# Ten, nine and seven instead of eight, twelve and six: where 26 weight conversions run in an attention, expert and mixing kernel

## The chip, the cores and the metric

One core of one Trainium2 chip. The metric is the time of one execution in microseconds (us) on the device. Before: 499.5 us, the median of 3 runs (498.26 to 500.18).

## What is computed

Three layers one after the other, on a batch of 2 sequences of 768 tokens, 8 heads of 64 (so 512 channels). First attention in a window with a few global positions; then a layer of 8 experts, in which every token goes through one expert chosen by a scan over the sequence; then a mixing layer. The last two matter here:

```python
# experts (E = 8, F = 1024); e is the expert of the token
h = np.maximum(x[b, s] @ w1[e], 0.0)
out[b, s] = p[e] * (h @ w2[e])

# mixing layer
theta = x @ w_theta
zr, zi = x * np.cos(theta), x * np.sin(theta)
y = np.einsum('ts,bsd->btd', w_tok_r, zr) + np.einsum('ts,bsd->btd', w_tok_i, zi)
u = x + y
return u + np.maximum(u @ w_ch, 0.0)
```

## The kernel before

The weights of the mixing layer (`w_theta`, `w_tok` and `w_ch`) come to the kernel as 64-bit numbers. Each has to be turned into two 32-bit parts, a high one in the format of the matmul and the rest, before PE can use it. This is cut into 26 conversions of 128 x 512 numbers, the list `jobs` (L358): 0 to 3 are `w_theta`, 4 to 21 `w_tok` (three for each of six slices of 128 tokens), 22 to 25 `w_ch`. Nothing needs them before the mixing layer, so most of them are slipped in among the work of the experts.

One conversion is the generator `job` (L396): an absolute value on ScalarE (ACT, L408) and a shift on VectorE (DVE, L409); three more DVE steps that put the 32-bit number together (L411, L413, L415), with a `yield` between the steps; a pause of `lag` yields; the copy of the high part on ACT (L418) together with the issue of a later load (`job_load`, L381); and the subtraction for the low part on DVE (L421). `job_tick` (L423) takes an open conversion one step further, or begins the next one if its data has been asked for. `job_upto(n)` (L433) ticks until n conversions have been begun and none is open.

The kernel is scheduled by hand: each engine runs its instructions in the order of the program, so a conversion step stands in the queue of DVE or ACT exactly where its tick is called.

The experts are one loop over 64 units (L1539), eight for each expert. The unit u does the second product of unit u (`mm2`) and the first of unit u + 2 (`mm1`) on PE, splits the next weights into two parts on ACT and DVE (`split_w1`, for the first four experts alone, and `split_w2`), and applies the relu. Between these stand five ticks. Whether a unit ticks is asked once, from the number of conversions begun and a due line: `NJ1` conversions over the units up to 32, `NJ2` over the 25 units after that, between `J0 = 6` and `JL = 61`. Here `lag` is 5, so a conversion takes 10 ticks, and the raw data has room for two. The loads of the expert weights are issued by the SP queue, those of the conversions by ACT's.

The mixing layer takes what is left (L1781). A pass k (1 to 11) on PE is: a quarter of the token product of slice k (`h_mix`, L1729), the theta product of slice k + 2 (L1653), the transposes of slice k + 3 (L1617), the other three quarters. The theta product and the transposes write PSUM tiles of one pool `pB` with two buffers in turn. On DVE and ACT a pass is `trig_a` (L1663 on ACT, L1665 to L1671 on DVE) that reads theta, `h_xh` and `h_xl` that read the transposes, then sine, cosine and the two-part factors `z` (L1704, L1709). In pass 5 `h_u` (L1741, L1748) takes the sums of the first batch out of their six PSUM banks, which the first quarter of pass 6 writes again. The ticks of a pass are 18, in three places (`T1`, `T2`, `T3` = 2, 2, 14), and each is worth `nj / JT` of a step, where `nj` is the number of conversions left and `JT` = 18. Here `lag` is 1, so a conversion takes 6 steps. At the beginning of passes 1 to 5 stands a `job_upto` (L1879), which makes sure that the slice's weights are there. The conversions of this part have three buffers for raw data; the first three loads are issued by ACT's queue, the rest by SP's.

Of the kernel before, what the change touches and what calls it, by code (L numbers as in the profile page):

```python
# [49 lines left out]
BLOCKS = [b * NT + t for t in range(NT) for b in range(B)]  # L50
TWO_PI = 6.283185307179586

NJ1, NJ2 = 8, 12
NWARM = 8
WPS = 1
TR_LAST = {}
# [1922 lines left out]
```

## Time and profile before

| | before |
|---|---|
| median of 3 runs | 499.5 us (498.26 to 500.18) |
| the profiled execution | 502.46 us, its span 500.6 us |
| PE busy | 475.2 us, 95% of the span |
| DVE busy | 348.0 us, 70% |
| ACT busy | 265.7 us, 53% |
| experts in the trace | about 133 to 318 us, their second half from about 232 us |
| mixing layer | about 318 to 500 us |

PE is TensorE, PEld its loading of weights, DVE is VectorE, ACT ScalarE, POOL GpSimd, SP the queue of SyncE. A name such as L415 is line 415 of the kernel. Times in the rows are microseconds from the start of the span. Busy time of PE includes matmuls that overlap, so a stretch in which PE has no idle time is one in which it sets the pace.

### The profile page before, as it was taken

The page shows a single profiled execution, that of the slowest core. Times are in us where ns is not written, and L with a number is a line of the kernel's source. Part 1 is how long each engine was busy: PE and PEld are TensorE (multiplying, and loading weights), DVE is VectorE, ACT ScalarE, POOL GpSimd, SP SyncE. Part 2 cuts the span into 40 slices and gives each one's busy share as a digit, 9 for nine tenths or more (in the row PEclk, how much of TensorE's full clock was granted, in tenths as well). Part 3 has the DMA queues.
Part 4 walks back from the last instruction along what each step waited for, and adds up shares of the span by engine and source line. Part 5 has one row for each costly group of instructions (what it writes and reads, how often), then busy time and mean ns, then how long its engine had stood idle before and what let it go on. Part 6 is the DMA issues. An engine that isn't in the chain of part 4 may idle for free.

```text
span 500.6 us, 9754 instructions
## 1 busy us (share of the span) xinstructions
PE 475.2 (95%) x3424; PEld 393.5 (79%) x3424; DVE 348.0 (70%) x963; ACT 265.7 (53%) x647; POOL 145.0 (29%) x164
## 2 busy tenths in 40 slices
PE   8888998999899899999999989999999999999997
PEld 4567776668788689788888767888888888888886
DVE  6687776855577897976799888556888787571522
ACT  4877877572345776564656556446555354340300
POOL 6535463421401330201312101212443244250300
PEclk9899999899999999999999999999999999999999
DMA  8547575188898998687999984150221000000022
GB/s 274 180 129 259 150 246 196 38 252 282 301 260 161 373 321 288 212 275 232 291 309 347 345 272 133 52 185 1 84 65 63 22 22 22 0 1 33 31 106 84
DMA packets 53252, 86.33 MB, mean 172 GB/s; under 512 B 6512, under 2 KB 28784, under 8 KB 53200
## 3 DMA queue, kind: packets, MB, share of 16 engines
q1 hardware_dynamic: 44068, 63.25, 38.8%
q10 hardware_dynamic: 6380, 15.50, 9.9%
q0 software_dynamic: 2752, 6.93, 4.9%
q8 instruction: 28, 0.46, 0.4%
q14 instruction: 24, 0.20, 0.1%
HBM read 71.17 MB, written 14.49 MB: 171 GB/s over the span
## 4 chain that ended last, share of the span: by engine, by line
PE 57%; DMA 7%; DVE 5%; ACT 2%; issue 1%; ACTq 0%; DVEq 0%
PE a L1729 20%; PE o L1458 9%; PE h L1419 7%; PE b L1766 7%; PE th L1653 6%; DMA jraw<-in_w_tokT_dram 4%; PE h L1403 4%; DMA raw<-in_w_dram 3%; PE o L1469 2%; DVE w2s L1387 1%; PE b L1617 1%; DVE jw L413 1%; PE tr L1258 1%; PE th L1818 1%; DVE jw L415 1%
## 5 line engine op out<-in xcount | busy, mean ns | idle before, releaser
L1729 PE MATMUL a<-wtok,z 128*128 128x512 f32 x576 | 105.4, 341 | 0.0
L1729 PEld LDWEIGHTS a<-wtok,z 128*128 128x128 f32 x576 | 88.5, 188 | 13.1 <-DVE z L1709 0.3
L1458 PE MATMUL o<-w2s,hh 128*128 128x512 f32 x192 | 66.1, 419 | 3.8 <-ACT w2s L1386 1.9
L1419 PE MATMUL h<-xT,w1s 128*128 128x288 f32 (+3 forms) x384 | 52.7, 285 | 4.5 <-DVE w1s L1284 3.3
L1419 PEld LDWEIGHTS h<-xT,w1s 128*128 128x128 f32 x384 | 49.1, 190 | 8.4 <-DVE w1s L1284 4.6
L623 ACT ACTIVATE pr<-sm,st 128x256 f32<-128x256 f32 (+1 forms) x96 | 46.0, 483 | 14.7 <-DVE xt L696 12.1
L1387 DVE TENSOR_TENSOR w2s<-raw,w2s 128x512 fp32r<-128x512 f32 x64 | 43.9, 687 | 4.7 <-ACT w2s L1386 4.3
L1403 PE MATMUL h<-xT,raw 128*128 128x192 f32 (+1 forms) x256 | 44.4, 317 | 0.9 <-issue 0.9
L613 DVE CUSTOM_DVE_ANT_0 sm<-s,bias 128x256 f32<-128x256 f32 (+1 forms) x96 | 34.2, 394 | 14.1 <-PE s L589 13.0
L1403 PEld LDWEIGHTS h<-xT,raw 128*128 128x128 f32 x256 | 39.6, 190 | 4.9 <-issue 3.0
L1386 ACT ACTIVATE w2s<-raw 128x512 fp32r<-128x512 f32 x64 | 39.8, 622 | 3.7 <-ACT yo L1508 1.8
L1458 PEld LDWEIGHTS o<-w2s,hh 128*128 128x128 f32 x192 | 32.6, 186 | 10.4 <-DVE w2s L1387 4.6
L1051 POOL DMA_INDIRECT xg<-xd,xidx x17 | 16.9, 994 | 80.4 <-PE tr L1258 57.8
L1458 PE MATMUL o<-w2s,hl 128*128 128x512 f32 x96 | 37.9, 395 | 0.0
L1433 ACT ACTIVATE hh<-h 128x128 fp32r<-128x128 f32 (+3 forms) x64 | 20.4, 319 | 30.4 <-PE h L1419 15.2
L646 PE MATMUL pt<-ident,pr 128*128 128x128 f32 x176 | 27.2, 286 | 4.3 <-ACT ps L655 3.7
L1685 POOL TENSOR_TENSOR si<-si,yg 128x512 f32<-128x512 f32 x10 | 13.5, 1353 | 59.2 <-ACT si L1678 50.0
L655 ACT ACTIVATE ps<-pt 128x512 f32<-128x512 f32 (+1 forms) x44 | 24.6, 559 | 6.9 <-PE pt L646 6.9
L1774 DVE SCALAR_TENSOR_TENSOR ob<-b,xTf 128x512 f32<-128x512 f32 (+1 forms) x16 | 8.8, 556 | 27.7 <-PE b L1766 27.7
L1284 DVE TENSOR_TENSOR w1s<-raw,w1s 128x512 fp32r<-128x512 f32 x32 | 22.0, 689 | 8.1 <-ACT w1s L1283 7.8
L646 PEld LDWEIGHTS pt<-ident,pr 128*128 128x128 f32 x176 | 20.1, 145 | 8.7 <-ACT ps L655 5.7
L670 PE MATMUL x<-ps,vv 128*64 128x128 f32 x352 | 25.5, 281 | 0.2 <-ACT ps L655 0.2
(264 smaller groups left out, 949.7 us busy)
## 6 DMA issues: line engine op xcount, KB each, us to landing
raw<-in_w_dram SPq DMA_DIRECT2D x64, 512.0 KB, 6.4
qk<-in_pack_dram SPq DMA_DIRECT2D x11, 576.0 KB, 6.0
jraw<-in_w_tokT_dram ACTq DMA_DIRECT2D x12, 512.0 KB, 6.0
vv<-in_pack_dram SPq DMA_DIRECT2D x10, 512.0 KB, 4.4
w<-in_w_dram SPq DMA_DIRECT2D x16, 256.0 KB, 5.6
yd<-zero SPq DMA_DIRECT2D x13, 256.0 KB, 3.0
xd<-xt SPq DMA_DIRECT2D x12, 256.0 KB, 4.6
jraw<-in_w_tokT_dram ACTq DMA_DIRECT2D x12, 256.0 KB, 4.9
```

Of the source, the lines that this page charges most:

```text
L613: V.tensor_tensor_reduce(out=sm[:, hh, 0:W], in0=ust[u]["s"][hh][:, 0:W], in1=bias[:, 2 * j + hh], scale=-0.125, scalar=BIG, op0=ALU.add, ...
L623: A.activation(pr[:, hh, 0:W], sm[:, hh, 0:W], AF.Exp, bias=st[:, hh : hh + 1], scale=-1.0, accum_out=sums[n][:, 2 * j + hh : 2 * j + hh + 1],
L646: PE.transpose(pt[:, hh, c], pr[:, hh, c * 128 : (c + 1) * 128], ident)
L670: PE.matmul(xp[64 * hh : 64 * hh + 64, j], lhsT=vv[:, i, h * 64 : (h + 1) * 64], rhs=ps[:, hh, c], start=(c == 0), stop=(c == nch - 1),)
L1386: A.activation(h2, bb[:, o], AF.Copy)
L1387: V.tensor_tensor(l2, bb[:, o], f32(h2), op=ALU.subtract)
L1403: PE.matmul(hp[:, :N], lhsT=pieces[u // 2][1][:, j, o * 128 : (o + 1) * 128], rhs=x[:, j, :N], start=(j == 0), stop=(j == 3),)
L1419: PE.matmul(hp[:, :N], lhsT=wa[:, j], rhs=xa[:, j, :N], start=(k == 0), stop=(k == 11))
L1458: PE.matmul(out[:M], lhsT=ha[:, lo : lo + M], rhs=wa, start=(f == 0 and q == 0), stop=(f == 7 and q == 2),)
L1653: PE.matmul(th, lhsT=xa[:, j], rhs=wa[:, j], start=(n == 0), stop=(n == 11))
L1729: PE.matmul(acc[b][d][o], lhsT=za[:, d * 128 : (d + 1) * 128], rhs=wa[:, c, lo:hi], start=(t == 0 and n == 0 and (o == 0 or d % 2 == 0)), ...
L1766: PE.matmul(op[:, : hi - lo], lhsT=wa[:, d, e * 128 : (e + 1) * 128], rhs=ua[:, d, lo:hi], start=(n == 0), stop=(n == 11),)
```

## The change

```diff
-NJ1, NJ2 = 8, 12
+NJ1, NJ2 = 10, 9
```

Nothing else is edited. `NJ1` and `NJ2` stand in the due line (L1541), in the limit of `job_load` (L383) and in the assertions at the end of the experts (L1593). Written out, with the ticks that the rule gives:

| | before | after |
|---|---|---|
| units with ticks, first half (6 to 31) | 6 to 10, 12, 13, 16, 17, 20, 21, 24, 25, 28, 29 | 6 to 14, 16, 17, 20, 21, 23, 24, 26, 27, 29, 30 |
| units with ticks, second half (32 to 57) | 32, 33, 35 to 57 | 32, 33, 35, 36, 38, 39, 41, 42, 44 to 47, 49, 50, 52, 53, 55 to 57 |
| conversions begun before unit 32 / in the experts | 8 / 20 | 10 / 19 |
| left for the mixing layer (`nj`) | 6 | 7 |
| steps in a pass of the mixing layer | 6 | 7 |

## Rows read from the trace of the kernel before

**Rows 1.** Busy time by stretch: us, PE, PEld, DVE, ACT, POOL, granted clock, DMA, GB/s

```profile
150.00:232.00 82.00, 78.61 (x535) 68.55 (x535) 66.22 (x123) 52.52 (x108) 18.30 (x18) 1.00 0.88 275
232.00:310.00 78.00, 73.29 (x485) 60.32 (x484) 66.00 (x163) 45.44 (x100) 12.91 (x13) 1.00 0.84 279
343.40:390.50 47.10, 47.10 (x259) 40.29 (x258) 37.02 (x58) 25.52 (x45) 20.81 (x15) 1.00 0.18 57
...
165.00:185.00 20.00, 17.66 (x110) 14.96 (x109) 17.40 (x33) 14.08 (x29) 7.01 (x7) 1.00 1.04 356
```

**Rows 2.** Waits of PE, 150 to 232 us: us in total, times, longest

```profile
PE h L1419 <- DVE w1s L1284: 3.3, 4, 1.0
```

**Rows 3.** Waits of PE, 232 to 318 us

```profile
PE o L1458 <- ACT w2s L1386: 1.9, 2, 1.4
PE o L1458 <- DVE w2s L1387: 1.6, 4, 0.8
PE h L1403 <- issue: 0.9, 1, 0.9
```

**Rows 4.** Chain that ended last, mixing layer: start us, us, what

```profile
367.00 2.81 PE th L1653 x12
...
378.73 2.81 PE th L1653 x12
...
390.46 2.81 PE th L1653 x12
...
393.70 8.48 PE a L1729 x48
```

**Rows 5.** DVE in order of time, mixing layer: start, us, instruction, [idle before <- releaser]

```profile
361.73 0.69 DVE L1667 SCALAR_TENSOR_TENSOR rr<-kk,th 128x512 f32<-128x512 f32 x1
...
364.11 0.42 DVE L409 TENSOR_SCALAR jw<-jraw 128x512 int32<-128x512 int32 x1
...
366.62 0.69 DVE L411 SCALAR_TENSOR_TENSOR jw<-jraw,jw 128x512 int32<-128x512 int32 x1
367.46 1.54 DVE L1709 TENSOR_TENSOR z<-kk,z 128x512 fp32r<-128x512 f32 x1 [0.16 <-ACT z L1704]
368.92 0.68 DVE L413 SCALAR_TENSOR_TENSOR jw<-jraw,jw 128x512 int32<-128x512 int32 x1
369.63 0.69 DVE L415 SCALAR_TENSOR_TENSOR jw<-jm,jw 128x512 f32<-128x512 f32 x1
371.03 0.69 DVE L421 TENSOR_TENSOR wtok<-jw,wtok 128x512 fp32r<-128x512 f32 x1 [0.70 <-ACT wtok L418]
...
372.09 0.69 DVE L1667 SCALAR_TENSOR_TENSOR rr<-kk,th 128x512 f32<-128x512 f32 x1
...
382.66 0.69 DVE L1667 SCALAR_TENSOR_TENSOR rr<-kk,th 128x512 f32<-128x512 f32 x1
...
388.69 1.27 DVE L1709 TENSOR_TENSOR z<-kk,z 128x512 fp32r<-128x512 f32 x1 [0.44 <-ACT z L1704]
...
395.74 0.69 DVE L1741 TENSOR_TENSOR xTf<-a,xTf 128x512 f32<-128x512 f32 x1 [2.47 <-PE a L1729]
396.35 0.75 DVE L1748 TENSOR_TENSOR xTf<-a,xTf 128x256 f32<-128x256 f32 x2
```

**Rows 6.** DMA issues of the page: KB each, median us to landing

```profile
jraw<-in_w_tokT_dram ACTq DMA_DIRECT2D x12, 512.0 KB, 6.0
```

**Rows 7.** ACT, DVE and PE in order of time, second half of the experts

```profile
298.51 0.67 ACT L408 ACTIVATE jw<-jraw 128x512 f32<-128x512 f32 x1 [2.00 <-DMA jraw<-in_w_tokT_dram]
...
306.79 0.70 DVE L415 SCALAR_TENSOR_TENSOR jw<-jw 128x512 f32<-128x512 f32 x1
...
308.15 0.51 PE L1458 MATMUL o<-w2s,hh 128*128 128x512 f32 x1 [0.83 <-DVE w2s L1387]
```

**Rows 8.** DVE and PE in order of time, first half of the experts

```profile
209.97 0.69 DVE L415 SCALAR_TENSOR_TENSOR jw<-jw 128x512 f32<-128x512 f32 x1
...
211.32 1.49 PE L1419 MATMUL h<-xT,w1s 128*128 128x224 f32 x11 [1.04 <-DVE w1s L1284]
```

## The prediction

> **What bounds the kernel now.** I began with the busy time of the engines in three stretches [rows 1]. The reader is to see in them that TensorE (PE) is busy 78.61 of 82 us in the first half of the experts, 73.29 of 78 in the second and 47.10 of 47.10 in the last layer, at a granted clock of 1.00 throughout (the 2.4 GHz level), while VectorE (DVE) is the next busiest in all three. So PE is the floor, and a conversion can cost or give back only where PE waits. The waits of PE come next [rows 2, 3]: 3.3 us in the first half, all for `w1s` from DVE; 1.9 + 1.6 + 0.9 = 4.4 us in the second. For 326 to 497 us the same view lists none, and the chain of waits there is PE work end to end [rows 4]. Last I read DVE in order of time in the last layer [rows 5], because that gives the margin by which it runs ahead of PE.
>
> **What one conversion costs.** Its DVE instructions are L409 0.42 us, L411 0.69, L413 0.68, L415 0.69 and L421 0.69 [rows 5], together 3.17 us, plus two activations on ScalarE (ACT), L408 and L418, and one load of 512 KB that takes 6.0 us to land [rows 6]. The number of conversions in the kernel stays 26; all the change does is move them: two into the first half (+6.3 us of DVE), three out of the second (-9.5 us), one into the last layer (+3.2 us). Per-step dispatch, the number of loads and the engines that issue them stay, so these are costed at nothing.
>
> **Second half, three fewer.** Counting ticks by the rule at L1541, before has conversion steps in every unit from 35 to 57, after in 17 of these 23; in the last ten (48 to 57) before works on five conversions, after on about three and a half. In 232 to 310 us DVE is busy 66.00 of 78 us [rows 1], of which the twelve conversions are 12 x 3.17 = 38.0; without them PE would be far ahead as the bound, with them the two are near each other. The stalls have the conversion in front of them: at 306.79 us L415 ran ahead of the `w2s` subtraction (L1387) that PE then got at 308.15 after 0.83 us idle; at 298.51 us ACT had stood 2.00 us for `jraw` with the `w2s` copy queued behind it [rows 7]. In the last ten units the conversions ask 3.5 x 3.17 = 11.1 us of DVE where they asked 15.9, and most loads have three units instead of two until they are read. Bounds: at best all 4.4 us go, plus some 0.6 us by which single matmuls are stretched, 5.0; at worst what is left of the conversions still meets the output copies on ACT and half stays, 2.0. I take **-3.8 us**, near the upper end, because every one of the three waits has a conversion step or its load ahead of it.
>
> **First half, two more.** After has steps in units 6 to 14 without a gap, where before left out 11 and 14, and in ten of the units 11 to 24 instead of seven: 3 x 5 ticks, one and a half conversions, 4.8 us of DVE in less than half of the half. Over the whole of it DVE is busy 66.22 of 82 us [rows 1], 15.8 us idle, but part of that is waiting for ACT, which an in-order engine can't fill. The form of the stall is in the trace: L415 began at 209.97 us, the `w1s` subtraction stood behind it, and PE went on at 211.32 after 1.04 us idle [rows 8]. Two more conversions at such a stall each are 2.1 us. Bounds: 0.5 us if the idle time takes nearly all; 4.0 us if all but 0.8 of the 4.8 lands on PE. I take **+2.0 us**.
>
> **Last layer, one more: where I expect the change to be decided.** Six conversions shared by 18 ticks of a pass k give 6 steps a pass, and with a lag of 1 a conversion is exactly 6 steps: each begins and ends inside its pass. Seven give 7 steps: at the end of pass 1 the next conversion is begun (L409), and `job_upto` at L1879 doesn't only ask whether the number wanted has been begun, it runs on while a conversion is open. So passes 2, 3 and 4 each begin with the remaining five steps in one piece, ahead of `trig_a`; two conversions a pass instead of one, all seven done by pass 4 instead of pass 6. Each such piece, L409 included, holds DVE for 0.42 + 0.69 + 0.68 + 0.69 + 0.70 (the wait for ACT's copy) + 0.69 = **3.87 us** [rows 5]; behind it wait L1665 and all of `trig_a` on DVE, and on ACT the copy `kk`, since it stands behind L418.
>
> DVE has a margin to swallow this. It goes round in 372.09 - 361.73 = 10.36 us [rows 5], PE in 378.73 - 367.00 = 11.73 [rows 4]. The theta product of pass k+1 writes the PSUM tile (`pB`, two buffers shared with the transposes) that L1667 of pass k read last. Pass 2: L1667 ends at 361.73 + 0.69 = 362.42, theta begins at 367.00, margin 4.58; less 3.87 leaves 0.71, no wait. Pass 3: 378.73 - 372.78 = 5.95, less 7.74: PE waits 1.79. Pass 4: 390.46 - 383.35 = 7.11, less 11.61: 4.50 in all. Pass 5 evacuates the sums of the first batch: the bank that PE wants at 393.70 + 3/4 x 8.48 = 400.06 is free when L1748 ends, at 397.10. DVE's delay is then 11.61 less 2.47 (its idle before the second L1741, which it no longer has) and less 0.44 (its wait at 388.69, which was one for PE in the end) [rows 5], 8.70: 405.80 against 400.06 + 4.50, another 1.24. Sum **+5.7 us**. What is late next, the `z` parts, has more margin: pass 4's end at 388.69 + 1.27 = 389.96, 10.1 us before 400.06. From pass 5 on there is no conversion and DVE catches up behind PE. Bounds: nothing (even below it there is no gain, PE has no idle there to give back) if the tile is free earlier than I read; 8 us if each piece also delays GpSimd's share of `z` by a collision such as the 1.54 us that L1709 took at 367.46 where the like subtraction L421 took 0.69, 0.85 us in each of three passes [rows 5].
>
> **The sum.** -3.8 + 2.0 + 5.7 = +3.9 us. The profiled execution took 502.46 us (span 500.6), 2.96 above the median of 499.5; against it the sum is 506.4, against the median **503.4 us**.
>
> **Rivals.** (1) The last layer hides its extra conversion: not slower. For it: PE has no wait there now, and DVE's load is 37.02 of 47.10 us [rows 1], with room for 3.17 more on the average. Against it: the steps come in three pieces at the wrong place, not on the average. It decides where a piece costs under 7.11 / 3 = 2.4 us instead of 3.87, or the tile theta waits for is another. Then -3.8 + 2.0 = -1.8: 497.7 us, and 495 with the upper end of the second half's gain and the lower of the first half's cost. (2) The first half is bound by transfers. In 165 to 185 us the DMA engines are busy 1.04 of their time at 356 GB/s [rows 1]; the change brings two loads of 0.524 MB forward, each 0.524 / 356 = 1.5 us of all the engines, and the weights of the next units land that much later. That is 2.9 us on top of my 2.0, so 506.3 us. Against it: over the whole first half the share is 0.88 [rows 1], and the weights are fetched several units ahead. The Trainium skill ("DMA: Bandwidth & Descriptors", Issuing engines are not separate DMA queues) speaks for this rival and against the change: transfers from several issuing engines run on the same sixteen DMA engines and interleave, so that the conversions' loads from ACT's queue slow the weights of SP's. By it the sum is 506.3, with queues that don't touch each other 503.4; no row of the kernel before parts the two. (3) That the change doesn't do what it says is excluded by counting: 19 conversions end in unit 57, as 20 did, and the assertion at L1593 holds.
>
> **Chances.** About 0.5% of this time, 2.5 us, is what a measurement can tell from no change. Forecast 0.55 (slower by more than that 0.41, within 0.14), rival 1 0.30 (faster 0.12, within 0.18), rival 2 0.15 (slower). So faster 0.12, within 0.32, slower 0.56. The range takes in most of rival 1 and all of rival 2: 496.5 to 508.0 us.
>
> **What would show it.** Second half: PE's waits for `w2s` and `h` down from 4.4 us to about 1, ACT's waits for `jraw` nearly gone. First half: PE's waits for `w1s` up from 3.3 to about 5 us, new ones near units 11 to 16. Last layer: L411 to L421 in one piece ahead of L1665 in passes 2 to 4, the last conversion some 20 us earlier relative to PE, and PE idle before the theta products of passes 4 and 5 (as counted by the product they compute, k+2 = 6 and 7) and before the first sum of the second batch. If PE is gapless there, the step with the margin is wrong and rival 1 holds; if the first half's waits are for `raw` rather than for DVE, rival 2.

## The result: 502.6 us instead of 499.6

| | before | after |
|---|---|---|
| median of 4 runs each | 499.62 us (498.26 to 500.18) | 502.56 us (501.43 to 508.32) |
| ratio to before | | 1.0106, 95% interval 1.0065 to 1.0148 |
| the profiled execution | 502.46 us, span 500.6 | 502.07 us, span 500.3 |

The change makes the kernel slower by 2.9 us in the medians, 0.6%; the ratio of the runs is 1.1% (0.65 to 1.5). That it is slower is clear, by how much less so. The two profiled executions take the same time all the same. Their difference lies ahead of the change: the first product of the experts begins at 133.27 us in the trace of before and at 130.29 in the trace of after, and the code up to there is the same. In the fourteen traces of this document that product begins between 129.7 and 134.1 us. So I compare by stages, each measured from a mark in the trace. These are the marks, PE in order of time, first of before, then of after (start, us, instruction):

```profile
133.27 2.90 PE L1419 MATMUL h<-xT,w1s 128*128 128x288 f32 x20 [1.14 <-ACTq L1296]
...
231.61 1.46 PE L1403 MATMUL h<-xT,raw 128*128 128x192 f32 x8
...
320.24 3.13 PE L1818 MATMUL th<-wth,wch 128*128 128x256 f32 x24
```

```profile
130.29 5.29 PE L1419 MATMUL h<-xT,w1s 128*128 128x288 f32 x36 [1.14 <-ACTq L1296]
...
230.64 1.46 PE L1403 MATMUL h<-xT,raw 128*128 128x192 f32 x8
...
313.50 3.13 PE L1818 MATMUL th<-wth,wch 128*128 128x256 f32 x24
```

From one mark to the next, and to the end of the span:

| stage | before | after | difference | predicted |
|---|---|---|---|---|
| first half of the experts | 98.34 | 100.35 | +2.01 | +2.0 |
| second half | 88.63 | 82.86 | -5.77 | -3.8 |
| mixing layer | 180.36 | 186.80 | +6.44 | +5.7 |
| sum | 367.33 | 370.01 | +2.68 | +3.9 |

2.68 us agrees with the 2.94 of the medians. But each stage is read from one trace: the same code of the experts as in before took 86.83 us for its second half in another run (e2_pieces, below), and against that the gain there is 4.0 us and the sum +4.5.

The busy times of after, same columns as [rows 1] and beside them:

```profile
150.00:232.00 82.00, 77.37 (x522) 66.68 (x521) 68.92 (x130) 53.24 (x108) 17.91 (x17) 1.00 0.89 280
232.00:310.00 78.00, 77.48 (x541) 64.64 (x540) 62.65 (x161) 44.23 (x100) 13.11 (x13) 1.00 0.81 267
343.40:390.50 47.10, 43.77 (x229) 36.83 (x228) 38.09 (x61) 22.33 (x41) 14.83 (x11) 0.96 0.22 67
```

The second half has become almost gapless for PE (77.48 of 78 us, before 73.29), the first half a little thinner, and the mixing layer, which had no gap, has 3.3 us of them. The waits of PE in 150 to 232, 232 to 318 and 326 to 497 us, against [rows 2, 3] (us in total, times, longest):

```profile
PE h L1419 <- DVE w1s L1284: 3.6, 6, 1.0
PE h L1419 <- ACT w1s L1283: 0.9, 1, 0.9
...
PE o L1458 <- DVE w2s L1387: 0.2, 1, 0.2
PE h L1403 <- DVE hl L1438: 0.2, 1, 0.2
...
PE th L1653 <- DVE rr L1667: 3.3, 2, 2.5
```

The last line is the one that no row of before had: theta waits for the DVE instruction that reads the PSUM tile it is to write. What stands ahead of that instruction is seen on DVE in order of time, at the head of pass 2, where [rows 5] go from L421 on to `trig_a`:

```profile
353.96 0.69 DVE L421 TENSOR_TENSOR wtok<-jw,wtok 128x512 fp32r<-128x512 f32 x1 [0.70 <-ACT wtok L418]
354.56 0.42 DVE L409 TENSOR_SCALAR jw<-jraw 128x512 int32<-128x512 int32 x1
355.02 0.69 DVE L411 SCALAR_TENSOR_TENSOR jw<-jraw,jw 128x512 int32<-128x512 int32 x1
355.75 0.69 DVE L413 SCALAR_TENSOR_TENSOR jw<-jraw,jw 128x512 int32<-128x512 int32 x1
356.54 0.69 DVE L415 SCALAR_TENSOR_TENSOR jw<-jm,jw 128x512 f32<-128x512 f32 x1
357.93 0.69 DVE L421 TENSOR_TENSOR wtok<-jw,wtok 128x512 fp32r<-128x512 f32 x1 [0.70 <-ACT wtok L418]
358.55 0.42 DVE L1665 TENSOR_SCALAR kk<-kk 128x512 f32<-128x512 f32 x1
359.00 0.69 DVE L1667 SCALAR_TENSOR_TENSOR rr<-kk,th 128x512 f32<-128x512 f32 x1
```

From L409 to L1665 it is 358.55 - 354.56 = 3.99 us, a whole conversion in one piece, where before L1665 followed L421 at once. The same piece stands at 368.91 and at 383.59 us, ahead of the L1667 of passes 3 and 4:

```profile
373.69 0.69 DVE L1667 SCALAR_TENSOR_TENSOR rr<-kk,th 128x512 f32<-128x512 f32 x1
...
388.02 0.69 DVE L1667 SCALAR_TENSOR_TENSOR rr<-kk,th 128x512 f32<-128x512 f32 x1
```

PE answers with two waits (PE in order of time, first before, then after):

```profile
378.57 2.03 PE L1653 MATMUL th<-wth,xh 128*128 128x512 f32 x8
...
390.29 2.03 PE L1653 MATMUL th<-wth,xh 128*128 128x512 f32 x8
```

```profile
374.53 2.73 PE L1653 MATMUL th<-wth,xh 128*128 128x512 f32 x8 [2.50 <-DVE rr L1667]
377.06 1.91 PE L1653 MATMUL th<-wth,xl 128*128 128x512 f32 x4
...
388.86 2.10 PE L1653 MATMUL th<-wth,xh 128*128 128x512 f32 x8 [0.83 <-DVE rr L1667]
390.79 1.10 PE L1653 MATMUL th<-wth,xl 128*128 128x512 f32 x4
```

Counted from L1818, theta of pass 4 begins 2.70 us later than before (374.53 - 313.50 against 378.57 - 320.24), that of pass 5 5.31, that of pass 6 5.96 (401.24 against 402.02 us). The remaining 0.48 us of the layer's 6.44 lie behind its last product.

### The profile page after: what moved, and what is told of

It reads as the page before. It is cut to its first block, busy times and chain, and to the rows that moved or that the text cites. A ratio compares the mean times of both kernels' runs of the same rounds, so it can differ in the third digit from the quotient of the medians.

```text
span 500.3 us, 9748 instructions
## 1 busy us (share of the span) xinstructions
PE 474.6 (95%) x3421; PEld 392.5 (78%) x3424; DVE 348.4 (70%) x963; ACT 265.8 (53%) x647; POOL 144.6 (29%) x164
## 4 chain that ended last, share of the span: by engine, by line
PE 46%; DVE 14%; ACT 7%; DMA 3%; issue 2%; ACTq 1%; DVEq 0%
PE a L1729 11%; PE o L1458 9%; PE b L1766 7%; PE h L1419 6%; PE h L1403 5%; DMA raw<-in_w_dram 3%; PE th L1653 3%; PE o L1469 2%; DVE jw L413 2%; DVE z L1709 1%; DVE jw L415 1%; DVE w2s L1387 1%; DVE jw L411 1%; DVE kk L1692 1%; DVE rr L1669 1%
## 5 line engine op out<-in xcount | busy, mean ns | idle before, releaser
L1729 PE MATMUL a<-wtok,z 128*128 128x512 f32 x576 | 105.8, 341 | 0.1
L1729 PEld LDWEIGHTS a<-wtok,z 128*128 128x128 f32 x576 | 88.5, 188 | 13.7 <-issue 0.4
L1458 PE MATMUL o<-w2s,hh 128*128 128x512 f32 x192 | 64.9, 416 | 0.3 <-DVE w2s L1387 0.2
L1458 PE MATMUL o<-w2s,hl 128*128 128x512 f32 x96 | 37.9, 394 | 0.0
L1458 PEld LDWEIGHTS o<-w2s,hh 128*128 128x128 f32 x192 | 32.4, 186 | 5.3 <-DVE w2s L1387 1.7
L1653 PE MATMUL th<-wth,xh 128*128 128x512 f32 x88 | 23.3, 408 | 3.3 <-DVE rr L1667 3.3
```

The lines of the kernel that those rows point to most:

```text
L1458: PE.matmul(out[:M], lhsT=ha[:, lo : lo + M], rhs=wa, start=(f == 0 and q == 0), stop=(f == 7 and q == 2),)
L1653: PE.matmul(th, lhsT=xa[:, j], rhs=wa[:, j], start=(n == 0), stop=(n == 11))
L1729: PE.matmul(acc[b][d][o], lhsT=za[:, d * 128 : (d + 1) * 128], rhs=wa[:, c, lo:hi], start=(t == 0 and n == 0 and (o == 0 or d % 2 == 0)), ...
```

## The experiments

Theory A says that the mixing layer pays for the piece of steps which `job_upto` runs at the head of a pass; theory B that it pays for the seventh conversion itself. For the second half, theory D says that the DVE steps of the conversions cost, theory L that the waits for their loads do. The stages below are measured from the same marks, in one trace of each run. The ratio of a run is to executions of before that were timed beside it, whose medians were 498.1 to 499.9 us.

| run | conversions | first half | second half | mixing layer | median, ratio to before (95%) |
|---|---|---|---|---|---|
| before | 8, 12, 6 | 98.34 | 88.63 | 180.36 | |
| after | 10, 9, 7 | 100.35 | 82.86 | 186.80 | 502.56, 1.0106 (1.0065 to 1.0148) |
| e1_even | 10, 9, 7 | 100.13 | 82.80 | 180.84 | 496.63, 0.9968 (0.9944 to 0.9992) |
| e2_pieces | 8, 12, 6 | 98.83 | 86.83 | 185.36 | 504.00, 1.0112 (1.0075 to 1.0150) |
| e3_first_alone | 10, 12, 4 | 101.38 | 90.25 | 180.33 | 503.56, 1.0104 (1.0068 to 1.0141) |
| e4_second_alone | 8, 9, 9 | 98.05 | 87.25 | 190.76 | 507.18, 1.0180 (1.0136 to 1.0223) |
| e5_no_read_wait | 8, 12, 6 | 99.22 | 85.49 | 180.39 | 496.94, one run |
| e6_second_no_read_wait | 8, 9, 9 | 98.47 | 83.20 | 191.13 | 504.57, one run |
| e7_no_loads | 10, 9, 7 | 99.68 | 82.61 | 180.69 | 496.03, one run |
| e8_close_only_due | 10, 9, 7 | 100.82 | 82.84 | 180.83 | 496.42, 0.9941 (0.9912 to 0.9969) |
| e9_early_loads | 8, 12, 6 | 100.70 | 89.74 | 180.39 | 504.36, 1.0102 (1.0062 to 1.0141) |
| e10_combined | 8, 10, 8 | 102.73 | 84.94 | 180.75 | 499.54, 1.0013 (0.9983 to 1.0042) |
| e11_8_9_due | 8, 9, 9 | 98.87 | 85.72 | 189.33 | 507.85, 1.0173 (1.0134 to 1.0212) |
| e12_8_10_due | 8, 10, 8 | 98.49 | 85.52 | 180.83 | 496.43, 0.9950 (0.9914 to 0.9986) |

### The mixing layer: the piece, or the seventh conversion

The changed kernel with six steps a pass again:

```diff
-JT = 18
+JT = 21
```

> The changed kernel with one more edit: JT = 21 instead of 18, so that the seven conversions left for the mixing layer again get six steps a pass, and each begins and ends inside its pass; the experts are untouched. Theory A (the cost in the mixing layer is the piece of steps that job_upto runs at the head of a pass, because a conversion is open there): PE has no wait for L1667 in that layer, the layer takes the 180.4 us from its first theta product to the end that it took before instead of 186.8, and the kernel takes about 502.6 - 6.4 = 496.2 us, a ratio to before of 0.993. Theory B (the seventh conversion costs by its own DVE and ACT work and its load, wherever its steps stand): the same 3.17 us of DVE are still there, the waits stay, 501 to 503 us.

The layer took 180.84 us, with no wait of PE in it; the median is 496.63 us. Seven conversions, and 6.0 of the 6.4 us are gone: theory B falls, and the kernel is slightly faster than before, by 0.1 to 0.6%. The other 0.48 us are at the very end: from the end of the last DVE instruction to the end of the span it is 3.2 us in the five traces with four or six conversions left and 3.5 to 3.7 in the nine with seven to nine, e1 and after alike. So they don't come from the piece; what they are stays open.

The other way round, the kernel before with the pieces and without the seventh conversion:

```diff
-ticks = {"n": 0, "done": 0, "per": nj / JT}
+ticks = {"n": 0, "done": 0, "per": 7 / 18}
```

> The kernel before (8, 12 and six conversions in the mixing layer) with 7 steps a pass instead of 6, so that a conversion is open at the end of passes 1 to 3 and job_upto runs it out at the head of passes 2 to 4. No conversion is moved or added. Theory A: PE waits for L1667 before the theta products of passes 4 and 5, as in the changed kernel (3.3 us there, 5.3 us of delay with the matmuls that run slower behind the wait); pass 4 has no second conversion here, so nothing more before pass 6: 499.6 + 5.3 = 504.9 us, ratio 1.011. Theory B: six conversions as before, 499.6 us.

185.36 us, 5.0 more than before, and 504.0 us in all. The waits of PE in this layer:

```profile
PE th L1653 <- DVE rr L1667: 3.0, 2, 2.2
```

The same wait, 3.0 us of it, without one conversion added. Theta of pass 6 begins only 0.07 us later still than that of pass 5 (0.65 in the changed kernel): this run has no second conversion in pass 4. Last the condition itself, in the changed kernel:

```diff
-while jstate["k"] < n or jstate["gen"] is not None:
+while jstate["k"] < n or (jstate["gen"] is not None and jstate["k"] <= n):
     job_tick()
```

> The changed kernel with one edit in job_upto: an open conversion is run out only if it is one of the n asked for (k <= n). The seven conversions keep seven steps a pass and spread over passes 1 to 6 with no piece at the head of passes 2 to 4; DVE's round grows by a sixth of 3.87, 10.36 + 0.65 = 11.0 us, still under PE's 11.73. Theory A (the piece costs): no PE wait in the mixing layer, 180.4 to 180.9 us of it, the kernel within 1 us of the one with JT = 21 (496.6). Theory B (the share of steps or the seventh conversion costs): 186 us of it, 502 to 503 us.

180.83 us, no PE wait, 496.42 us. Seven steps a pass cost nothing as long as they aren't closed into one piece. Busy times of the layer in this run:

```profile
343.40:390.50 47.10, 47.10 (x259) 40.22 (x258) 39.57 (x62) 24.85 (x44) 18.92 (x14) 1.00 0.23 73
```

DVE is busier than in the changed kernel (39.57 us against 38.09) and PE has no gap. It is not DVE's load that stopped PE but where the load stood.

### The second half: DVE steps, or waits for the loads

Two runs meant to do one half alone:

```diff
-NJ1, NJ2 = 8, 12
+NJ1, NJ2 = 10, 12
-JT = 18
+JT = 12
```

> The first half alone: NJ1, NJ2 = 10, 12, and JT = 12 so that the four conversions left take six steps a pass. From the first expert product to the first product of the fifth expert (L1403): 100.3 us as in the changed kernel instead of 98.3; the second half 88.6 us as before, with PE waits of about 4.4 us; the mixing layer 180.4 us. Sum 499.6 + 2.0 = 501.6 us, ratio 1.004. If the first half's 2.0 us between the two profiles were chance or came from the later stages: 499.6 us.

```diff
-NJ1, NJ2 = 8, 12
+NJ1, NJ2 = 8, 9
-JT = 18
+JT = 27
```

> The second half alone: NJ1, NJ2 = 8, 9, and JT = 27 so that the nine conversions left take six steps a pass; job_upto then runs one whole conversion at the head of pass 5 and one at the head of pass 8, where DVE is 8 us and more ahead. The first half 98.3 us as before, the second 82.9 us as in the changed kernel instead of 88.6. Theory A: no PE wait in the mixing layer in spite of nine conversions, 499.6 - 5.8 = 493.8 us, ratio 0.988. Theory B: three more conversions there cost about 6.4 us each, some 507 to 513 us.

Both missed. The first half of the first was as expected or somewhat more (+3.0), but its second half, which has before's twelve conversions, took 90.25 us, with 9.5 us of waits for `jraw` on ACT and DVE. And the second run, with the nine conversions of the changed kernel in the same units, gave back 1.4 us instead of 5.8. Its mixing layer is a flaw of my own design: the last of the three conversions of slice 5 runs at the head of pass 5, which uses them, and PE stood for it:

```profile
PE a L1729 <- ACT wtok L418: 7.6, 1, 7.6
```

That is a missed due time and says nothing on A or B. What it says on the second half is in the chain of waits (start, us, what):

```profile
261.79 9.90 DMA jraw<-in_w_tokT_dram
...
271.71 0.68 ACT jw L408
272.39 0.53 ACT w2s L1386
```

A load asked for at 261.79 us landed 9.90 us later. ACT stood 2.54 us for it, and the `w2s` copy that PE needs stood behind. ACT and DVE waited for such loads 8.6 us in this half of that run, 7.6 us in before, 1.1 in the changed kernel (ACT, 230 to 314 us):

```profile
ACT jw L408 <- DMA jraw<-in_w_tokT_dram: 1.1, 2, 0.7
```

So part of the half's gain is not DVE time at all. To part the two, the loads went on at their places, but nobody read them (they also go to DRAM here and not to the buffer of before, so the traffic isn't quite the same):

```diff
+d = jstate["dummy"][:, k] if jstate["room"] and k > 1 else t
-jstate["eng"].dma_start(t[:, o : o + n], src...)
+jstate["eng"].dma_start(d[:, o : o + n], src...)
...
+jstate["dummy"] = dram.tile([128, 20, 512, 2], I32, name="jdummy", tag="jdummy")
```

> The kernel before (8, 12), in which the loads of conversions 2 to 19 are still issued at the same places and sizes, but go to a buffer in DRAM that nobody reads, and these conversions work on the data of the first two; so it leaves out converting the right weights, and keeps every DVE and ACT step and nearly the same traffic. Theory D (the second half lost its time because twelve conversions ask too much of DVE): second half 87 to 89 us as before, PE waits about 4 us. Theory L (it lost it because a conversion's first step stood for its load on ACT and DVE, 7.6 us in all, with the w2s copies behind it): no such waits, second half about 84 us, PE waits under 1.5 us.

> The same edit (loads issued but not read, conversions 2 and on work on the data of the first two, which leaves out converting the right weights) on the kernel with 8 and 9. That one took 87.25 us for the second half with 8.6 us of waits for loads, though its nine conversions stand in the same units as those of the changed kernel, which took 82.86. Theory L: 82.5 to 83 us, as the changed kernel. Theory D: it can't tell the two kernels apart by the waits; the half stays at about 87 us. The mixing layer keeps its wait of 7.6 us in either.

With twelve conversions and no read of a load the half took 85.49 us, and the waits of PE left in it are

```profile
PE o L1459 <- DVE w2s L1388: 2.1, 5, 0.8
```

(the line numbers are one higher there). With nine it took 83.20, close to the 82.8 us of the changed kernel. Neither theory alone: 88.63 - 85.49 = 3.1 us of before's half go with the waits for loads, 85.49 less 82.6 to 83.2 = 2.3 to 2.9 us with the three conversions' steps in front of PE's operands. These are differences of single traces, but the other runs fall in line. With twelve conversions, 0, 4.3, 7.6 and 9.5 us of waits for loads go with halves of 85.49 (e5), 86.83 (e2), 88.63 (before) and 90.25 us (e3); with nine, 0 to 1.1 us with 82.80 to 83.20 (e6, e8, e1, after), 5.4 us with 85.72 (e11) and 8.6 us with 87.25 (e4). With ten (e12) it was 6.9 us and 85.52.

So nine conversions don't by themselves avoid the waits. It isn't chance either: in e4 and in e11 the load asked for 32.40 us after the half's first mark lands 9.90 and 9.99 us later, and ACT stands for it 2.5 and 2.6 us. The waits are few in the three runs in which ten conversions came before (after, e1, e8); why the loads of those land in time stays open.

If the loads come late, issue them earlier? In the experts, after the first pause tick instead of the last:

```diff
-for _ in range(jstate["lag"]):
+for i in range(jstate["lag"]):
+    if i == 1:
+        job_load()
     yield
 A.activation(wh, wf, AF.Copy)
-job_load()
+if jstate["lag"] == 1:
+    job_load()
```

> The kernel before (8, 12, six in the mixing layer), with one edit in job: in the experts a conversion issues the load of a later one after the first of its five pause ticks, not after the last, some four ticks (0.8 of a unit, about 2 us) earlier; the raw data was read for the last time by L413 before that. Twelve conversions in the second half as before. Theory D and L together (12 conversions cost that half about 2.6 us by their DVE steps and 1.3 to 3.1 us by waits for their loads): the waits for loads mostly go, second half about 85.5 us as without the read, mixing layer 180.4, the kernel 1 to 3 us under before, ratio 0.994 to 0.998. Theory D alone: second half 87 to 89 us, ratio 1.000.

Slower, 504.36 us; the first half grew as well, to 100.70 us. The waits for loads are gone, and others stand in their place (waits of ACT, second half):

```profile
ACT hh L1436 <- DVE jw L413: 5.2, 3, 2.3
ACT w2s L1389 <- DVE jw L413: 5.2, 2, 2.7
```

The load overwrites what L413 reads, so its issue waits for L413, and it is ACT's queue that waits, with the relu and the `w2s` copy behind it. In this trace the longest semaphore instruction at the issue (L391) takes 2.80 us; in before, with the issue after the pause, none of ACT's there takes more than 0.02 us.

### The first half: transfers or DVE steps

The changed kernel with even steps, and without the loads:

```diff
-jstate["eng"].dma_start(t[:, o : o + n], ...)
+if not jstate["room"] or k < 2:
+    jstate["eng"].dma_start(t[:, o : o + n], ...)
```

> The changed kernel with JT = 21, and without the loads of conversions 2 to 18 (they work on the data of the first two, so converting the right weights is left out): 8.9 MB less to move in the experts. For the first half, rival 2 (transfers): the weights land earlier, and of its 100.1 us about 2 to 4 go, 96 to 98 us. My reading (DVE): PE's waits for w1s behind the steps of a conversion stay, 99.5 to 100.5 us. Second half: 82.9 us and little else, since its waits are gone already.

99.68 us. The five runs with eight conversions and no edit to the loads took 98.1 to 98.9 us (before, e2, e4, e11, e12), the four with ten 100.1 to 101.4 (after, e1, e3, e8). Taking out the loads of all seventeen conversions from 2 on gave back 0.4 to 1.1 us (100.13 to 100.82 less 99.68), in a single run, and the half still lies 0.8 us above the slowest of these five (0.5 above e5, which has eight and the loads sent elsewhere). At least that much is the steps; how the rest of the 2.0 is shared isn't shown. The stalls for `w1s` stay: after, e1 and e7 have the same seven near 167, 168, 172, 176, 180, 198 and 228 us (in e7 one of them is listed under `xT`), 4.5, 4.4 and 4.0 us in sum, where before has four and 3.3 us.

### What the runs point to

> What the runs point to, in one kernel: NJ1, NJ2 = 8, 10 (the first half keeps its eight, 98.3 us), the earlier loads, and job_upto that runs out an open conversion only if it is asked for, with eight conversions left at eight steps a pass (DVE's round 10.36 + 2/6 of 3.87 = 11.65 us, just under PE's 11.73). Theory A with D and L: second half about 83.5 us, mixing layer 180.4 to 181 with no PE wait, 499 - 5 = 494 us, ratio 0.988 to 0.992. If the number of conversions in the mixing layer costs after all: 182 us and more there, ratio above 0.994.

> 8 and 9 in the experts, as in the run of the second half alone, with job_upto that runs an open conversion out only if it is asked for; nine conversions at nine steps a pass begin early enough for slice 5 (five of them within four passes, 36 steps). The half's own question: if the 87.25 us with 8.6 us of waits for loads come from the order in which reads meet loads, they come again (86.5 to 88); if they were chance, 82.9 as in the changed kernel. Mixing layer: DVE's round 10.36 + 3/6 of 3.87 = 12.3 us against PE's 11.73, over six passes 3.4 us of its margin of 4.6 to 7: no PE wait, 180.4 to 181 us, and none for the weights. In sum 494 to 498 us.

> 8 and 10 with the same job_upto and the loads at their old place: the combined run without its earlier loads. First half 98.4 us as before (the combined run took 102.7, with ACT standing at the earlier load for L413 and L415); if that half stays above 101 us the earlier loads were not its cause. Second half between 83 and 87 us. Mixing layer 180.4 to 181 us with eight conversions. In sum 494 to 498 us.

The combined run took 499.54 us, not 494: its mixing layer is right (180.75 us with eight conversions), but the earlier loads cost its first half 4 us; without them (e12_8_10_due) that half is back at 98.49 us and the kernel at 496.43 us. With nine conversions in the mixing layer (e11_8_9_due, 507.85 us) PE stood again, now for the weights of slice 5 (PE in order of time):

```profile
390.45 0.67 PE L1729 MATMUL a<-wtok,z 128*128 128x512 f32 x2 [3.66 <-ACT wtok L418]
393.70 3.57 PE L1729 MATMUL a<-wtok,z 128*128 128x512 f32 x10 [2.58 <-DVE wtok L421]
```

Counted in steps they were converted in time; but DVE runs most of a pass behind PE (theta of pass 4 begins at 377.03 us, the L1667 that reads it at 386.16), and the third conversion of slice 5 stands in its queue in pass 4; its last step begins at 392.97 us. I had counted ticks where I should have counted when DVE gets to them. The medians of e1, e8 and e12 lie within 0.2 us of each other, and all three are under the executions of before beside them; the intervals of their ratios don't part them.

## Why the prediction was right, point by point

The direction, the size (503.4 us predicted, 502.6 measured) and the place were right. That the size came so close is in part luck: the second half gave more than forecast and the mixing layer cost more, and the two errors have opposite signs. The mechanism in the mixing layer came out step by step: one open conversion at the end of a pass, `job_upto` running it out, pieces of 3.99 us where 3.87 were worked out, no wait in pass 3 and waits of PE ahead of theta in passes 4 and 5. Experiments from both sides (e1, e8 and e2) show that it is the piece.

Sizes were off in two terms of three.

- Theta of pass 4 was to be 1.79 us late and was 2.70, that of pass 5 4.50 and was 5.31. With L1818 as the common mark the L1667 of passes 2, 3 and 4 is late by 4.01, 8.34 and 12.10 us, where the sum had 3.87, 7.74 and 11.61; 0.46 us of it is a wait of DVE inside the second piece (at 371.24 us, ahead of L415). The margins were 5.79 and 6.94 us instead of 5.95 and 7.11, since PE in order of time begins theta 0.16 us before the chain of [rows 4] does, and from the end of L1667 to theta it takes another 0.15 us. 8.34 - 5.79 + 0.15 = 2.70 and 12.10 - 6.94 + 0.15 = 5.31: the delay is wholly that of DVE, which waits nowhere for PE between these L1667. The listed waits of PE are only 3.3 of these 5.3 us, mostly because PE ran slower behind the first one, told below, and so had less left to wait at the second. For pass 6, 1.24 us more were predicted and 0.65 came. They stand in no listed wait: the 48 matmuls of L1729 around the first sum of the second batch took 9.32 us instead of 8.73 (PE in order of time, before and after):

```profile
393.45 8.73 PE L1729 MATMUL a<-wtok,z 128*128 128x512 f32 x48
```

```profile
392.08 9.32 PE L1729 MATMUL a<-wtok,z 128*128 128x512 f32 x48
```

- The second half gave 5.8 us instead of 3.8, more than my upper bound of 5.0; against the trace of e2, with the same experts as before, it gave 4.0. I bounded it by the 4.4 us in which the view lists PE as waiting, plus 0.6 for stretched matmuls. The marks show that the stage shrank by 1.4 us more than the listed waits: PE's busy time fell as well, from 83.90 to 82.32 us for the same matmuls (599 and 598 in the traces), 1.2 us of it at L1458. I take this for matmuls that wait for an operand inside a group and count as busy, which no run shows by itself; in any case the listed waits are not the most that a stage can give back. The share of loads in it was seen in the rows but not priced by itself; e5 did that. My reason for it, three units instead of two until a load is read, isn't enough: e4 and e11 have the same units and kept 8.6 and 5.4 us of waits.
- The first half came out at 2.01 us for 2.0, in good part by the conversions' steps, as argued. Its listed waits rose by only 1.2 us, PE's busy time by 0.8. Rival 2 (transfers, 2.9 us more) falls with the 2.01 and with e7, in which the loads of seventeen conversions are worth 1.1 us at most.

Rival 1, that the layer hides its extra conversion, was wrong as the change was made and right as a statement on the seventh conversion: with its steps spread out, the layer hides it but for the 0.48 us at its end (e1, e8). The margin was counted to within 0.2 us; what the rival lacked was only the piece.

## What to carry to other kernels

A helper that closes what is open, put where a deadline may need it, turns into a block of work in front of a loop body as soon as the steps no longer divide evenly; ask of such a call what it does when nothing is due. The margin of a two-buffer PSUM ring is the time from the last reader of a tile to the next writer, and work put ahead of the reader draws on it pass after pass: sum it up before you spread the load "on the average". And work that reads a DMA in an in-order queue can cost, beside its own time, the lateness of the load, so count how long a load really takes under traffic before placing the read.

## What was not expected of the hardware

Behind the 2.50 us in which PE stood, its granted clock fell to the lower of its two levels. Busy times of after by small stretches (PE, PEld, DVE, ACT, POOL, then granted clock):

```profile
374.00:375.00 1.00, 0.47 (x2) 0.46 (x3) 0.96 (x2) 0.06 (x1) 0.00 (x0) 1.00 0.01 4
375.00:376.00 1.00, 1.00 (x5) 0.81 (x5) 0.97 (x3) 0.40 (x1) 0.00 (x0) 0.87 0.00 0
376.00:377.00 1.00, 1.00 (x3) 0.78 (x3) 0.50 (x2) 0.97 (x3) 0.69 (x1) 0.50 0.00 0
...
380.00:382.00 2.00, 2.00 (x13) 1.77 (x12) 1.97 (x3) 0.00 (x0) 1.66 (x2) 1.00 0.00 0
```

0.50 is 1.2 GHz, 1.00 is 2.4 GHz. The theta product there took 2.73 + 1.91 us where it takes 2.03 + 1.10, 1.5 us more behind a wait of 2.5; behind the wait of 0.83 us the clock stayed at 1.00 in every microsecond from 388 to 392, and the product took 2.10 + 1.10. In e2_pieces the product behind the first wait, of 2.16 us, took 2.83 + 1.91 us as well, at a clock of 0.50 from 379 to 382 us. So a wait on PE can cost more than it lasts. Here it didn't: the next theta waited for DVE in any case, and the slow product only made that second wait shorter.

The other is how late a 512 KB load can land: 6.0 us in the median of before's issues [rows 6], 9.90 us in the case shown above, and 9.99 at the same place in e11. The DMA engines were busy 0.88 of the time around it (255 to 275 us of the first of these runs), but 0.84 and 0.88 in the two halves of before too [rows 1], so the share alone doesn't explain it.
